# Queries and keys with eight tokens in a row of a partition, transposed head by head

## The chip, the cores and the metric

The kernel runs on one core of a Trainium2 chip. The metric is the device time of one execution in microseconds (us), from the first to the last instruction with what lies around them. Five engines work beside each other: TensorE (PE, matmuls; its weight loads are listed apart as PEld), VectorE (DVE), ScalarE (ACT), GpSimd (POOL) and SyncE (SP, which here only issues transfers). Sixteen DMA engines move the data.

## What is computed

Blockwise causal attention for 8 batches of 8 heads, 576 tokens, 64 values a head, followed by a mixture of experts with one expert a token:

```python
scores = scale * np.matmul(q, k.transpose(0, 1, 3, 2))      # q, k, v: (8, 8, 576, 64) float32
scores = np.where(block_i >= block_j, scores, -1e9)         # blocks of 64 tokens
attn = softmax(scores);  x = attn @ v                       # to (8, 576, 512)
...
e = argmax(x @ w_gate) where the local gate says so, else the expert of the token before
out = p[e] * (relu(x @ w1[e]) @ w2[e])
```

The change touches only the way in which q and k reach TensorE. Scores need both with the 64 values of a head on the partitions and the tokens along the free dimension, so each is loaded with tokens on the partitions and turned by TensorE.

## The kernel before

The attention part works on 32 pairs of heads (`NPR`), four pairs to a batch. It is a software pipeline: the loop `for it in range(-2, NPR)` (L979) handles in one iteration pair `a = it + 2` (turned), `c = it + 1` (maxima and scores), `e = it` (scores, exponentials, products with v) and `x = it - 1` (results stored and turned for the gate). The order of instructions on each engine is the order of the program text; nothing reorders it. After the loop, from about 303 us, come the experts' matmuls, whose weights were loaded during the attention part.

One pair's queries and keys lie in one half of `natb`, a tile [128, 2, 9, 2, 64] in f32 with two buffers: keys on partitions 64 to 127, queries on 0 to 63, then nine blocks of 64 tokens, two heads, 64 values. `load_qk` (L480) fills the first eight blocks. For every pair but the first it issues four transfers on SP, one for queries or keys (`w`) and head (`h`); partition si gets the tokens si, si + 64, si + 128 and so on, 256 B each. The ninth block comes from `load_ends` (L501). `load_qk(a + 2)` is issued when the banks of pair a have been copied out.

In `turns` (L1010) `turn_pair` (L991) transposes the eight blocks for both halves of the partitions: 16 transposes of [64 tokens, 2 x 64 values] into two PSUM banks `pw[0]` (queries) and `pw[1]` (keys), each [128, 512]: 64 partitions for each head, 512 tokens along the row. Pair 0 has its own path on all 128 partitions (L1014 to L1020). ACT copies both banks to `pl` (`turned_in`, L1024 to L1029); copies in bf16 go to `kh` and `qh` (`halves_in`, L1031), from which `top` (L578) computes rough scores, whose maxima DVE takes (L599). `products` (L651, f32), `less` (L659) and `expo` (L668) give the exponentials, `av` (L683) the products with v.

On PE one iteration runs, in order: the middle maxima's scores (L588, L594, L568), two segments of products (L655, L664), the turns (L993), the high maxima's scores (L573), products for the next pair (L655), the tails and the transposes of results (L717, L1050), the low maxima's scores (L573), `less` (L664) and `av` (L689, L697). Once a batch come the gate's sums (L762).

SP issues, each iteration, three transfers for v (L513, L515), the four of `load_qk`, two of `load_ends`, and the rows of x (L533, L538, L540). The experts' weights come through POOL's queue (L63).

Of the kernel before, what the change touches and what calls it, by code (L numbers as in the profile page):

```python
# [16 lines left out]
def kernel(  # L17
# [11 lines left out]
    nc = tc.nc  # L29
# [57 lines left out]
    def rt(shape, dt, name):  # L87
        return rt_p.tile(shape, dt, tag=name, name=name)

    id_f = rt([P, P], F32, "id_f")  # L90
# [352 lines left out]
    with tc.manual_schedule():  # L443
# [33 lines left out]
            "p (m z s d) -> p m z s d", z=2, s=2, d=D)  # L477
        NTWO = NPR - 6

        def load_qk(i, engs=(nc.sync,)):  # L480

            b, hp = divmod(i, HP)
            t = nats[i] = natb[:, i % 2]
            if i:
                for w in (1, 0):
                    for h in range(2):
                        nc.sync.dma_start(out=t[64 * w:64 * w + 64, 0:8, h, :],
                                          in_=(q, k)[w][b, 2 * hp + h, :512].rearrange(
                                              "(so si) d -> si so d", si=64))
                return  # L490
            for z, (w, h) in enumerate(((1, 0), (1, 1), (0, 0), (0, 1), (1, 2), (0, 2))):
                s = (q, k)[w][b, 2 * hp:2 * hp + 2]
                eng = engs[z % len(engs)]
                if h < 2:
                    eng.dma_start(out=t[:, 4 * w:4 * w + 4, h, :],
                                  in_=s[h, :512].rearrange("(so si) d -> si so d", si=128))
                else:
                    eng.dma_start(out=t[64 * w:64 * w + 64, 8],
                                  in_=s[:, 512:S].rearrange("h p d -> p h d"))
# [106 lines left out]
        def rows(h):  # L606
            return slice(64 * h, 64 * h + 64)
# [272 lines left out]


        load_qk(0, (nc.sync, nc.scalar))
        nc.scalar.copy(share[:, 0:1], ones[:, 0:1])
        load_qk(1)
        load_ends(1)
        warm(26)
# [92 lines left out]
        for it in range(-2, NPR):  # L979
# [4 lines left out]
            if it == 0:  # L984
                nc.sync.dma_start(out=wgl[:, :, :E],
                                  in_=moe_w_gate.rearrange("(do di) e -> di do e", di=P))
                for ko in range(KO1):
                    nc.sync.dma_start(out=wgl[:, ko, E:E + 1],
                                      in_=moe_w_local[ko * P:(ko + 1) * P, :])

            def turn_pair(b):  # L991
                for w in range(2):
                    nc.tensor.transpose(pw[w][:, 64 * b:64 * b + 64],  # L993
                                        nat[rows(w), b].rearrange("p h d -> p (h d)"),
                                        id_f[rows(w), rows(w)])

            def weights(n):
                while n:
# [11 lines left out]
            def turns():  # L1010

                pw[:] = g_tile(0), g_tile(1)
                if a == 0:
                    for w in (1, 0):  # L1014
                        for t in range(4):
                            nc.tensor.transpose(pw[w][:, 128 * t:128 * t + 128],
                                                nat[:, 4 * w + t].rearrange("p h d -> p (h d)"),
                                                id_f)
                        turned(0, w, pw[w])
                    return  # L1020
                for b in range(8):
                    turn_pair(b)
# [61 lines left out]
            pw = []  # L1084
            if on_a:
                nat = nats[a]
                pl = pls[a] = plb[:, a % 2]
                mxs[a] = o_p.tile([P, 16], F32, tag="mx", name="mx")
            if it == -2:
                turns()  # L1090
                g1 = tails()
                tails_in()
                load_qk(2)
                load_ends(2)
                top(0, 2, 1)
                low_exchange(0)
                weights(2)
                mid_maxima(0, 2)
                low_shift(0)
                opened = seg_tile(0)  # L1100
                products(0, opened, 0, 0)
                products(0, opened, 0, 1)
                high_maxima(0, 1)
                continue
# [307 lines left out]
```

## Time and profile before

| | |
|---|---|
| median of three runs | 449.35 us (447.96 to 454.55) |
| the profiled execution | 452.64 us, of it 450.9 us from the first to the last instruction |
| granted TensorE clock in it | 0.998 |
| attention part | to about 303 us |
| HBM read and written | 67.18 MB and 14.97 MB |

How to read the rows below: a row of the groups names line, engine, operation, the tile written and the tiles read, the shape (partitions and columns of the array by `64*128`, then partitions x elements), the count, busy us, and the mean ns of one instruction, which on PE includes its way through the array, so that many overlap. A row of the chain of work gives start, duration, engine, tile and line of a piece; the chain is followed back from the last instruction to what released each step. A row of the windows gives for a stretch the busy us of each engine with counts, the granted clock, the share of the DMA engines and GB/s. A row of the timeline gives the start of a merged group and the time to its last end.

### The profile page before, as it was taken

To read this page: it belongs to the slowest core of one execution; us is meant where nothing else is said; L and a number is where in the kernel's file an instruction comes from. 1 tells how busy PE (TensorE), PEld (TensorE's weight loads), DVE (VectorE), ACT (ScalarE), POOL (GpSimd) and SP (SyncE) were. 2 spreads that over 40 slices of the span, in tenths; PEclk is the share of its full clock that TensorE was granted. 3 is DMA by queue.
4 is the path that set the end of the run, shared out by engine and by line. 5 is a ranking of instruction groups with operands and counts; after the bars stand their busy time and mean duration, and the time that the engine had idled before them with its cause. 6 is when DMAs were issued, how large, how long until landed. Compare 5 with 4: busy or idle time off the path is not lost.

```text
span 450.9 us, 19788 instructions
## 1 busy us (share of the span) xinstructions
PE 431.3 (96%) x7802; PEld 338.7 (75%) x7802; DVE 316.2 (70%) x842; ACT 271.0 (60%) x573; POOL 294.2 (65%) x699
## 2 busy tenths in 40 slices
PE   7999999999999999999999999999999999999994
PEld 6687787878787887788778877886776776767772
DVE  5777667768778878897999898857966862433332
ACT  4766665766567757775676666554554553545452
POOL 4656457657556566787766788664777667676752
PEclk9999999999999999999999999999999999999999
DMA  8999689999999997989888898857545746455541
GB/s 154 195 156 188 127 171 183 172 184 165 192 168 172 170 178 152 192 168 186 160 163 172 152 186 159 153 108 165 144 140 154 145 126 156 124 152 145 144 132 63
DMA packets 169887, 71.18 MB, mean 158 GB/s; under 512 B 151424, under 2 KB 158080, under 8 KB 169792
## 3 DMA queue, kind: packets, MB, share of 16 engines
q1 hardware_dynamic: 154640, 38.05, 44.4%
q0 software_dynamic: 13952, 31.52, 34.1%
q8 instruction: 65, 1.06, 1.0%
q10 hardware_dynamic: 1200, 0.30, 0.3%
q14 instruction: 30, 0.25, 0.2%
HBM read 67.18 MB, written 14.97 MB: 182 GB/s over the span
## 4 chain that ended last, share of the span: by engine, by line
PE 61%; DVE 11%; DMA 9%; issue 7%; POOL 6%; ACT 4%; POOLq 1%; ACTq 0%; DVEq 0%
PE g L697 13%; PE ps_s L655 12%; PE ps_h L828 10%; PE ps_o L843 8%; DVE mx L599 5%; PE g L689 4%; DMA out_dram<-o_sb,tok2s 3%; PE ps_s L664 3%; DMA x_rows<-w_bf 2%; PE g L762 2%; PE g L993 2%; POOL out_dram L852 2%; PE ps_m L573 1%; DMA vt<-in_v_dram 1%; PE g L717 1%
## 5 line engine op out<-in xcount | busy, mean ns | idle before, releaser
L671 ACT ACTIVATE prob<-ps_s 128x640 f32<-128x640 f32 (+2 forms) x128 | 103.6, 839 | 45.8 <-PE ps_s L664 42.5
L599 DVE TENSOR_REDUCE mx<-ps_m 128x2 f32<-128x640 f32 (+2 forms) x96 | 100.2, 1044 | 15.2 <-PE ps_m L594 5.6
L655 PE MATMUL ps_s<-plb 64*128 64x320 f32 (+4 forms) x768 | 103.8, 391 | 0.5 <-DVE mx L604 0.2
L655 PEld LDWEIGHTS ps_s<-plb 64*128 64x128 f32 x768 | 68.6, 187 | 21.2 <-issue 11.0
L697 PE MATMUL g<-vt,prob 128*64 128x65 f32 x2560 | 81.5, 222 | 1.1 <-issue 1.1
L697 PEld LDWEIGHTS g<-vt,prob 128*64 128x64 f32 x2560 | 78.1, 138 | 1.8 <-issue 1.7
L843 PE MATMUL ps_o<-w_bf,hT 128*128 x304 | 71.5, 379 | 0.0
L832 ACT ACTIVATE hT<-ps_h 128x512 bf16<-128x512 f32 x76 | 44.0, 597 | 42.1 <-PE ps_h L828 31.1
L809 DVE COPY natb<-w_bf 128x4096 bf16 x20 | 24.7, 1234 | 38.5 <-PE ps_h L828 24.2
L843 PEld LDWEIGHTS <-hT 128*128 128x128 bf16 x304 | 28.0, 98 | 27.8 <-issue 0.3
L846 ACT ACTIVATE o_sb<-ps_o,share 128x512 f32<-128x512 f32 x37 | 25.4, 687 | 28.7 <-PE ps_o L843 14.3
L828 PEld LDWEIGHTS <-plb 128*128 128x128 bf16 x608 | 35.5, 98 | 7.2 <-issue 3.2
L828 PEld LDWEIGHTS <-natb 128*128 128x128 bf16 x608 | 35.4, 98 | 4.6 <-issue 0.7
L664 PE MATMUL ps_s<-diag,ones 64*128 64x448 bf16 (+2 forms) x372 | 37.1, 274 | 1.3 <-DVE diag L618 0.6
L809 DVE COPY plb<-w_bf 128x4096 bf16 x20 | 24.8, 1241 | 15.9 <-PE ps_h L828 13.9
L63 POOL DMA_DIRECT2D w_bf<-in_moe_w_dram x56 | 34.1, 609 | 1.5 <-DMA x_rows<-xb 0.4
L1029 ACT COPY plb<-g 128x512 f32<-128x512 f32 x62 | 33.2, 593 | 0.2
L681 POOL MEMSET prob<- 64x128 f32 x128 | 24.2, 205 | 12.8 <-ACT prob L671 7.4
L612 POOL COPY mx<-mx 64x2 f32<-64x2 f32 x64 | 11.9, 185 | 31.4 <-DVE mx L599 29.8
L852 POOL DMA_INDIRECT out_dram<-o_sb,tok2s x17 | 21.0, 1237 | 16.5 <-ACT o_sb L846 9.1
L689 PEld LDWEIGHTS g<-vt,prob 128*64 128x64 f32 x640 | 21.4, 137 | 10.6 <-ACT xT L725 4.5
L689 PE MATMUL g<-vt,prob 128*64 128x65 f32 x640 | 26.0, 227 | 3.4 <-ACT xT L725 1.2
(290 smaller groups left out, 801.8 us busy)
## 6 DMA issues: line engine op xcount, KB each, us to landing
w_bf<-in_moe_w_dram POOLq DMA_DIRECT2D x48, 256.0 KB
vt<-in_v_dram SPq DMA_DIRECT2D x64, 128.0 KB
natb<-in_k_dram SPq DMA_DIRECT2D x63, 128.0 KB
natb<-in_q_dram SPq DMA_DIRECT2D x63, 128.0 KB
w_bf<-in_moe_w_dram POOLq DMA_DIRECT2D x8, 512.0 KB
x_rows<-w_bf SPq DMA_DIRECT2D x13, 256.0 KB
natb<-in_k_dram SPq DMA_DIRECT2D x32, 32.0 KB
vt<-in_v_dram SPq DMA_DIRECT2D x32, 32.0 KB
```

The source lines that it names most:

```text
L63: nc.gpsimd.dma_start(out=dst[:, e * WE:(e + 1) * WE].rearrange("p (k f) -> p k f", k=n)[:, r:r + m, :], in_=view[e][:, r:r + m, :])
L599: nc.vector.reduce_max(mx[:, 7:12:4] if job == 0 else mx[:, b:b + 2], ps[:, :, 0:w], axis=AX)
L655: nc.tensor.matmul(ps[:, h, c:c + n], lhsT=pls[i][rows(h), S + 128 * j:S + 128 * j + 128], rhs=pls[i][rows(h), a:a + n], start=part == 0, ...
L664: nc.tensor.matmul(ps[:, h, c:c + n], lhsT=ones[rows(h), :], rhs=diag[rows(h), a // 64:(a + n) // 64, :], start=False, stop=part == len(SE ...
L671: nc.scalar.activation(p[:, :, SEG0[s]:SEG0[s] + w], ps[:, :, 0:w], func=AF.Exp, scale=scale_attn)
L689: nc.tensor.matmul(g[rows(h), 130:195], lhsT=p[:, h, c:c + 64], rhs=t[:, j, h, :], start=(j == 0), stop=(j == 4))
L697: nc.tensor.matmul(g[rows(e), o + 65 * h:o + 65 * h + 65], lhsT=p[:, h, c:c + 64], rhs=t[:, j, h, :], start=(j == 0), stop=(j == m))
L809: nc.vector.tensor_copy(w, w1_bf[:, bass.ds(off, WE)])
L828: nc.tensor.matmul(ps_h[:, f, :], lhsT=w[:, f0 + ko * F:f0 + ko * F + 2 * P - 1:2], rhs=xb[:, ko * P:(ko + 1) * P], start=(ko == 0), stop= ...
L832: nc.scalar.activation(hT[:, half * 4:half * 4 + 4, :], ps_h, func=AF.Relu)
L843: nc.tensor.matmul(ps_o, lhsT=hT[:, fo, :], rhs=w2_bf[:, bass.ds(woff + fo * Dm, Dm)], start=(fo == 0), stop=(fo == FO - 1))
L1029: nc.scalar.copy(pl[:, w * S:w * S + 512], pw[w])
```

## The change

The transfers of `load_qk` (for all pairs but the first) and `turn_pair` are rewritten; everything else stays.

```diff
+        def by_head(t):
+            return t[:, 0:8].rearrange("p s h d -> p (s h d)").rearrange("p (h n) -> p h n", h=2)
...
                 for w in (1, 0):
-                    for h in range(2):
-                        nc.sync.dma_start(out=t[64 * w:64 * w + 64, 0:8, h, :],
-                                          in_=(q, k)[w][b, 2 * hp + h, :512].rearrange(
-                                              "(so si) d -> si so d", si=64))
+                    nc.sync.dma_start(out=by_head(t)[64 * w:64 * w + 64],
+                                      in_=(q, k)[w][b, 2 * hp:2 * hp + 2, :512].rearrange(
+                                          "h (si so) d -> si h (so d)", so=8))
...
             def turn_pair(b):
-                for w in range(2):
-                    nc.tensor.transpose(pw[w][:, 64 * b:64 * b + 64],
-                                        nat[rows(w), b].rearrange("p h d -> p (h d)"),
-                                        id_f[rows(w), rows(w)])
+                for h in range(2):
+                    for w in range(2):
+                        nc.tensor.matmul(pw[w][rows(h), b:512:8],
+                                         lhsT=by_head(nat)[rows(w), h, 64 * b:64 * b + 64],
+                                         rhs=id_f[rows(w), rows(w)], start=True, stop=True)
```

The same 4 KB of a partition now hold, for each of the two heads, eight consecutive tokens (8 si to 8 si + 7) as one run of 2 KB, read from one run of 2 KB in memory. One transfer brings both heads, 256 KB. A turn b takes the b-th token of each of the 64 partitions, of one head, and puts them in every eighth column of the bank, so that the banks hold the tokens in the same order as before. Input and output of such a turn are 64 partitions each, a quarter of the array; it is an f32 matmul with the identity in place of a transpose. There are 32 of them for a pair in place of 16 transposes.

## The prediction

> **What bounds the kernel now.** I read the page first (span, slices, the shares of the chain of work that ended last), then the windows by stage, then the chain over one iteration, and last the groups by shape.
>
> ```profile
> span 450.9 us, 19788 instructions
> ...
> PE 431.3 (96%) x7802; PEld 338.7 (75%) x7802; DVE 316.2 (70%) x842; ACT 271.0 (60%) x573; POOL 294.2 (65%) x699
> ...
> PE 61%; DVE 11%; DMA 9%; issue 7%; POOL 6%; ACT 4%; POOLq 1%; ACTq 0%; DVEq 0%
> PE g L697 13%; PE ps_s L655 12%; PE ps_h L828 10%; PE ps_o L843 8%; DVE mx L599 5%; PE g L689 4%; DMA out_dram<-o_sb,tok2s 3%; PE ps_s L664 3%; DMA x_rows<-w_bf 2%; PE g L762 2%; PE g L993 2%; POOL out_dram L852 2%; PE ps_m L573 1%; DMA vt<-in_v_dram 1%; PE g L717 1%
> ```
>
> PE is busy for 96% and makes up 61% of the chain, transfers 9%. The lines of the change are L993 (2% of the chain) and the loads, which stand on the chain nowhere.
>
> ```profile
> 20.00:56.00 36.00, 34.71 (x740) 28.28 (x737) 25.35 (x65) 23.30 (x53) 20.28 (x68) 1.00 0.94 163
> 56.00:92.00 36.00, 35.59 (x792) 29.41 (x790) 25.76 (x67) 24.59 (x56) 23.16 (x75) 1.00 1.00 176
> 92.00:128.00 36.00, 34.58 (x750) 28.14 (x744) 27.49 (x75) 23.76 (x54) 22.71 (x74) 1.00 1.02 177
> ...
> 237.00:274.00 37.00, 35.83 (x776) 29.34 (x776) 33.85 (x99) 25.10 (x59) 27.61 (x86) 1.00 0.91 171
> ```
>
> The columns are PE, PEld, DVE, ACT, POOL busy, granted clock, DMA share, GB/s. In the attention stage PE works up to 35.6 of 36 us with the DMA engines at 1.00 beside it; late in the stage DVE (33.9 of 37) comes close. One iteration of the chain (start, duration) shows what PE does:
>
> ```profile
> 82.53 0.80 PE g L689 x20
> 83.33 2.33 PE g L697 x80
> ...
> 87.39 0.49 PE g L993 x16
> 87.89 0.22 PE ps_m L573 x2
> 88.11 1.68 PE ps_s L655 x16
> 89.78 0.31 PE g L717 x10
> ...
> 90.79 0.21 ACT scr L725
> ...
> 91.04 0.80 PE g L689 x20
> ```
>
> An iteration takes 91.04 - 82.53 = 8.51 us and is a row of PE pieces without a hole, closed by ACT's copies after the tails. The sixteen transposes of turn_pair (L993) hold 0.49 of it. Whatever they cost more is added to the iteration, unless another engine is later anyway.
>
> **The change part by part.** First, what the new turn is made of.
>
> ```profile
> L697 PE MATMUL g<-vt,prob 128*64 128x65 f32 x2560 | 81.5, 222 | 1.1 <-issue 1.1
> ...
> L655 PE MATMUL ps_s<-plb 64*128 64x320 f32 x256 | 44.2, 430 | 0.0
> ...
> L993 PE MATMUL g<-id_f,natb 64*128 64x64 f32 x496 | 20.9, 222 | 0.1
> ...
> L664 PE MATMUL ps_s<-diag,ones 64*128 64x320 bf16 x124 | 18.6, 296 | 0.0
> ...
> L573 PE MATMUL ps_m<-kh,qh 64*128 64x512 bf16 x64 | 12.2, 376 | 0.2
> ...
> L762 PE MATMUL g<-xT,wgl 128*32 128x160 f32 x64 | 5.9, 305 | 0.0
> ...
> L709 PE MATMUL g<-id_f,x 128*64 128x64 f32 x4 | 0.3, 246 | 0.0
> ```
>
> A transpose is one instruction: 31 turned pairs (the first pair has its own path) x 16 = 496. An f32 matmul, an identity one too, is two: L709 is called twice in the whole kernel and shows x4, and L697 is 32 pairs x 40 calls x 2 = 2560. So 16 transposes become 32 matmuls of a quarter of the array, 64 instructions with 64 weight loads, 16 for each quarter.
>
> What one costs, and how many run at once, is read in the timeline (start, span of the merged group):
>
> ```profile
> 85.32 0.34 PE L697 MATMUL g<-vt,prob 128*64 128x65 f32 x6
> 85.59 0.20 PE L588 MATMUL ps_m<-kh,qh 64*128 64x64 bf16 x2
> ```
> ```profile
> 58.59 0.47 PE L762 MATMUL g<-xT,wgl 128*32 128x160 f32 x8
> ```
>
> Eighty L697 in 2.33 us are 29 ns each; as its two column halves work side by side, one half takes 58 ns for 65 columns. The L762 row has eight matmuls of about 0.3 us inside 0.47 us: two rounds of four, on four column strips at once. Quarters (two row halves by two column halves) appear nowhere. The bounds: all four at once, 16 rounds x 58 = 0.93 us; two at once, 32 x 58 = 1.86 us. I take 0.93, since both kinds of halves and even four strips overlap here, and each half of the rows then streams what L697 streams. Removed: 0.49.
>
> Next, the shape of the array changes before and after the turn (now 64*128 like its neighbours L664 and L573). The six L697 above are three pairs (0.34 - 0.222 = two steps of 58 ns), the last from 85.44; the next would have been due at 85.50, but L588, of another shape, begins at 85.59: 0.09 to 0.10 us lost. Two such changes are new: +0.19 (bounds 0, if a quarter counts as the same shape, and 0.2). [...]
>
> So a turn goes from 0.49 to 1.12: +0.63 us on PE. What is queued behind it on PE is the top job (L573) and the products (L655); ACT waits with its copies out of the turned banks (L1026 to L1029), and POOL and DVE behind those; all move by the same amount.
>
> How many of the 31 pay? The chain holds 2.0% of 450.9 = 9.0 us of L993, 18 turns of 0.49. In the other 13 another engine is later, for example:
>
> ```profile
> 243.24 0.38 PE L573 MATMUL ps_m<-kh,qh 64*128 64x512 bf16 x2
> ```
> ```profile
> 244.44 1.14 DVE mx L599
> ```
>
> PE has the scores that this maximum reads at 243.62, DVE takes them up at 244.44: 0.82 us of room, as DVE is busy with other work. Room in the 13 lies between 0 and 0.82; I take 0.5, nearer to this row. Sum: 18 x 0.63 + 13 x 0.13 = 11.3 + 1.7 = 13.0 us (bounds for the room: 11.3 and 19.5).
>
> Then the loads. Four transfers a pair become two, 512 runs of 256 B each become 128 of 2 KB.
>
> ```profile
> q1 hardware_dynamic: 154640, 38.05, 44.4%
> q0 software_dynamic: 13952, 31.52, 34.1%
> ...
> natb<-in_k_dram SPq DMA_DIRECT2D x63, 128.0 KB
> ```
> ```profile
> L487 SPq DMA_DIRECT2D natb<-in_k_dram x62: 595/626/1218, 2.7 to 264.3; - x62
> ```
>
> 31 x 4 x 512 = 63488 of the queue's 154640 packets become 31 x 2 x 128 = 7936. A packet of q1 costs 0.444 x 16 x 450.9 / 154640 = 20.7 ns for 246 B; q0's, 2.26 KB on average, 176 ns. Per byte these are alike, so a 2 KB run may save nothing, or up to most of 63488 x 20.7 / 16 = 82 us of each engine; SP saves two issues of 0.63 us a pair. Either way the loads stand off the chain. What a lighter queue can reach are three pieces in which something else waited for a transfer:
>
> ```profile
> 31.63 6.04 DMA vt<-in_v_dram
> ...
> 43.84 5.16 DMA x_rows<-w_bf
> ...
> 115.27 5.88 DMA x_rows<-w_bf
> ```
>
> Here PE mostly went on with other work: in the windows 20 to 56 and 92 to 128, which hold the three pieces, it was idle 1.3 and 1.4 of 36 us, against 0.4 in 56 to 92. So at most 0.9 + 1.0 = 1.9 us can come back; I take 0.8 of 0 to 1.9, since the turns that grow fill part of the same holes. Nothing changes after 303 us, where the loads are over. Sum: +13.0 - 0.8 = +12.2. The profiled execution took 452.64 us, span 450.9, so it would take 464.8; the median of the three runs is 3.3 us below that execution, so I forecast 449.35 + 12.2 = 461.5 us.
>
> **The rivals.**
> Issue. The new turn wants 128 PE instructions in 0.93 us, 7 ns each. The narrowest stream of the trace is slower:
>
> ```profile
> 330.29 0.67 PE g L391 x27
> ```
>
> That is 25 ns for a matmul with its load, so 64 need 1.6 us. A turn then costs 1.6 + 0.19 - 0.49 = +1.30: 18 x 1.30 + 13 x 0.80 - 0.8 = +33, 482 us. Against it: L391 uses the whole array, and where two row halves take turns, six short matmuls start between 85.59 and 85.69, 17 ns each:
>
> ```profile
> 85.59 0.23 PE L588 MATMUL ps_m<-kh,qh 64*128 64x64 bf16 x4
> 85.66 0.19 PE L594 MATMUL ps_m<-kh,qh 64*128 64x64 bf16 x2
> 85.69 0.19 PE L568 MATMUL ps_m<-ones,unseen 64*128 64x64 bf16 x2
> ```
>  [...]
>
> Slow columns. The outputs are strided, every eighth f32 of a bank; every PE output of the trace lies in runs. If a strided column costs twice, 16 rounds cost 16 x 116 = 1.86 us, which is also the case of two quarters at once: +1.56 a turn, 18 x 1.56 + 13 x 1.06 - 0.8 = +41, 490 us. [...] For the other side: f32 columns come slowly already, (430 - 222) / 255 = 0.8 ns each by the rows of L655 and L697, against (376 - 296) / 192 = 0.4 for the bf16 ones of L573 and L664, so there may be time for one write each.
>
> No change. The shape change costs nothing and the queue's relief is whole: 18 x 0.44 - 1.9 = +6.0, 455 us (+1.3%), the 13 others absorbing 0.44 within 0.5.
>
> Faster. The full DMA engines set the pace after all, and the three pieces above, 17.1 us of the chain, vanish: 449.35 - 17.1 + 7.9 = 440 us. It decides only if all of the 17.1 goes; PE busy for 34.7 and 34.6 of 36 us in the windows that hold them speaks against.
>
> **How the numbers follow.** Quarters concurrent with two shape changes: 43 in 100, 461.5 us, own range 458 to 469. Issue 15 (482), slow columns or two at once 20 (490), no change 18 (455), faster 4 (440). The range 453 to 490 leaves out faster, the lowest part of no change and what would lie above both upper bounds. A measurement here tells about 2% (9 us) from no change. Faster by over 2%: 0.04; within 2%: 0.20 (no change, and the low edge of the first); slower by over 2%: 0.76.
>
> **What would show it.** The turn's line with 31 x 64 = 1984 matmuls, PE with 7802 + 1488 = 9290; the turn's piece of the chain about 1.1 us from the last L664 to the top job: 1.0 would take the shape changes away, 1.8 or more speaks for issue (if even starts 25 ns apart) or for slow columns (if each quarter's own step is above 58 ns). An undisturbed iteration goes from 8.51 to 9.1 us. q1 falls to 99088 packets; if the three transfer pieces stay, the lighter queue was worth nothing. Wrong it would be above all if the quarters do not overlap, or if iterations get shorter although PE does more.

## The result, and the profile after

The changed kernel takes 470.03 us against 448.26 us for the kernel before, medians of seven runs each; the ratio is 1.0446 (95% interval 1.0401 to 1.0492). Run again it came to 1.0501 (1.0472 to 1.0530), 477.82 against 455.24 us. It is slower by 20 to 23 us. The ratios take only the runs at the usual clock, and as the first profile of the changed kernel was taken at a granted clock of 0.655, the rows below are those of the second run, e0_after, at 0.996 (span 473.5 us). Its lines are numbered two to three higher than before. Beside it stands a second profile of the kernel before (b0_before, span 452.2 us). It comes from another chip than e0_after, but the kernel before takes 455.24 us in the median on the one and 455.29 on the other.

The page of the changed kernel:

```profile
span 473.5 us, 22616 instructions
...
PE 448.7 (95%) x9268; PEld 351.1 (74%) x9290; DVE 319.4 (67%) x842; ACT 273.7 (58%) x573; POOL 296.3 (63%) x699
...
q1 hardware_dynamic: 98096, 38.05, 36.9%
q0 software_dynamic: 13952, 31.52, 33.7%
q8 instruction: 76, 1.25, 1.1%
...
PE 68%; issue 12%; POOL 7%; ACT 5%; DMA 3%; DVE 3%; POOLq 1%; another core or an unknown queue 1%; DVEq 0%; ACTq 0%
PE ps_s L657 18%; PE g L699 15%; PE g L996 7%; PE g L691 5%; PE ps_h L830 4%; POOL out_dram L854 3%; PE ps_o L845 3%; DMA out_dram<-o_sb,tok2s 3%; PE ps_m L575 2%; PE ps_s L666 2%; POOL scr L795 2%; PE g L764 2%; PE g L719 2%; POOL xg L795 2%; ACT plb L1062 2%
```

The same of b0_before:

```profile
q8 instruction: 65, 1.06, 1.0%
...
PE 62%; issue 10%; DVE 8%; POOL 8%; DMA 6%; ACT 5%; POOLq 1%; ACTq 0%; DVEq 0%
```

PE issues 9290 weight loads in place of 7802, the 1488 more that were worked out, and the turn's line is 7% of the chain in place of 2% (3% in b0_before). DVE has gone from 11% of the chain (8% in b0_before) to 3%, and transfers from 9% (6%) to 3%. "Issue", time in which the engine waits for nothing that the profile shows, is 12% where the two profiles of before have 7% and 10%; between 20 and 300 us it is 2.4% of the chain, against 2.3% in b0_before, so most of it lies behind the part that was changed. The queue q1 has 56,544 packets fewer.

One plain iteration of the chain, to be held against the one of before:

```profile
63.64 1.09 PE g L996 x64
64.73 0.32 PE ps_m L575 x2
65.06 1.68 PE ps_s L657 x16
66.73 0.31 PE g L719 x10
...
67.18 0.27 ACT plb L1062
...
67.99 0.80 PE g L691 x20
68.80 2.33 PE g L699 x80
...
72.86 1.09 PE g L996 x64
```

It takes 72.86 - 63.64 = 9.22 us; it was 8.51. All other pieces are as long as before. The turn went from 0.49 to 1.09, and the piece of the top job behind it from 0.22 to 0.32. That is +0.70 us in every plain iteration, one in which no other engine is late.

The windows (PE, PEld, DVE, ACT, POOL busy, clock, DMA share, GB/s), first of the kernel before (b0_before), then of the changed one:

```profile
56.00:92.00 36.00, 35.61 (x784) 29.38 (x780) 26.29 (x68) 24.81 (x57) 23.12 (x73) 1.00 1.02 177
92.00:128.00 36.00, 35.42 (x775) 29.11 (x774) 29.57 (x77) 24.94 (x58) 23.71 (x76) 1.00 0.99 184
```
```profile
56.00:92.00 36.00, 34.75 (x884) 28.26 (x880) 23.41 (x62) 21.97 (x50) 21.05 (x68) 1.00 0.82 159
92.00:128.00 36.00, 35.12 (x890) 28.53 (x888) 26.68 (x70) 23.89 (x55) 21.46 (x69) 1.00 0.83 167
```

The DMA engines, which looked full at 1.02 and 0.99, are at 0.82 and 0.83, and nothing became faster by it. PE is idle for 1.25 us in the first of these windows, against 0.4 before: part of the loss is holes in PE's work, which e4_twice and e6_shift are about.

### The profile page after: what moved, and what is told of

Same layout as the page of the kernel before. It is cut to its first block, busy times and chain, and to the rows that moved or that the text cites. A ratio compares the mean times of both kernels' runs of the same rounds, so it can differ in the third digit from the quotient of the medians.

```text
span 632.4 us, 22638 instructions
## 1 busy us (share of the span) xinstructions
PE 624.3 (99%) x9290; PEld 449.9 (71%) x9290; DVE 324.6 (51%) x842; ACT 276.7 (44%) x573; POOL 290.0 (46%) x699
## 3 DMA queue, kind: packets, MB, share of 16 engines
q8 instruction: 76, 1.25, 0.8%
## 4 chain that ended last, share of the span: by engine, by line
PE 86%; issue 6%; DMA 4%; POOL 3%; POOLq 0%; DVE 0%; ACTq 0%; DVEq 0%
PE ps_s L657 21%; PE g L699 17%; PE ps_h L830 10%; PE ps_o L845 10%; PE g L996 7%; PE ps_s L666 5%; PE g L691 5%; PE ps_m L575 3%; DMA out_dram<-o_sb,tok2s 3%; PE g L764 2%; PE g L719 2%; PE ps_m L596 1%; POOL out_dram L854 1%; POOL xg L795 1%; PE ps_m L590 1%
## 5 line engine op out<-in xcount | busy, mean ns | idle before, releaser
L657 PE MATMUL ps_s<-plb 64*128 64x320 f32 (+4 forms) x768 | 148.8, 520 | 0.0
L657 PEld LDWEIGHTS ps_s<-plb 64*128 64x128 f32 x768 | 77.9, 200 | 45.4 <-issue 19.8
L699 PEld LDWEIGHTS g<-vt,prob 128*64 128x64 f32 x2560 | 109.2, 176 | 0.3 <-issue 0.3
L845 PE MATMUL ps_o<-w_bf,hT 128*128 x304 | 105.4, 512 | 0.0
L830 PEld LDWEIGHTS <-natb 128*128 128x128 bf16 x608 | 49.8, 119 | 8.0 <-issue 5.9
L830 PEld LDWEIGHTS <-plb 128*128 128x128 bf16 x608 | 50.0, 119 | 7.5 <-issue 6.1
L996 PEld LDWEIGHTS g<-id_f,natb 64*64 64x64 f32 x1984 | 41.5, 170 | 18.4 <-issue 18.1
L666 PE MATMUL ps_s<-diag,ones 64*128 64x448 bf16 (+1 forms) x372 | 47.6, 356 | 0.0
L996 PE MATMUL g<-id_f,natb 64*64 64x64 f32 x1984 | 47.4, 257 | 0.0
L614 POOL COPY mx<-mx 64x2 f32<-64x2 f32 x64 | 11.6, 181 | 70.9 <-DVE mx L601 69.4
L1037 POOL CAST qh<-plb 128x512 bf16<-128x512 f32 x30 | 18.3, 609 | 48.8 <-ACT plb L1032 48.8
L830 PE MATMUL ps_h<-scr,natb 128*128 128x128 bf16 x416 | 36.3, 265 | 0.0
```

What stands on the lines that cost most here:

```text
L657: nc.tensor.matmul(ps[:, h, c:c + n], lhsT=pls[i][rows(h), S + 128 * j:S + 128 * j + 128], rhs=pls[i][rows(h), a:a + n], start=part == 0, ...
L666: nc.tensor.matmul(ps[:, h, c:c + n], lhsT=ones[rows(h), :], rhs=diag[rows(h), a // 64:(a + n) // 64, :], start=False, stop=part == len(SE ...
L699: nc.tensor.matmul(g[rows(e), o + 65 * h:o + 65 * h + 65], lhsT=p[:, h, c:c + 64], rhs=t[:, j, h, :], start=(j == 0), stop=(j == m))
L830: nc.tensor.matmul(ps_h[:, f, :], lhsT=w[:, f0 + ko * F:f0 + ko * F + 2 * P - 1:2], rhs=xb[:, ko * P:(ko + 1) * P], start=(ko == 0), stop= ...
L845: nc.tensor.matmul(ps_o, lhsT=hT[:, fo, :], rhs=w2_bf[:, bass.ds(woff + fo * Dm, Dm)], start=(fo == 0), stop=(fo == FO - 1))
L996: nc.tensor.matmul(pw[w][rows(h), b:512:8], lhsT=by_head(nat)[rows(w), h, 64 * b:64 * b + 64], rhs=id_f[rows(w), rows(w)], start=True, sto ...
```

## The experiments

**e0_after.** The changed kernel, no edit.

> The changed kernel as it is, for a profile at a full granted clock. Turn theory (PE's longer turn makes all of the loss): ratio to before 1.045 as measured; the piece from the last L666 to the top job's first L575 is 1.1 us against 0.49, and a plain iteration goes from 8.51 to 9.1 us. Rival, the loads (2 KB runs cost time somewhere, or relieve it): the turn's piece is 1.1 us but the iterations or the waits for vt and x_rows change by more than that. Rival, the clock: the granted clock stays under 0.99 and the experts' part, which the change does not touch, is longer too.

Ratio 1.0501. A group row and a row of the timeline show how the quarters run:

```profile
L996 PE MATMUL g<-id_f,natb 64*64 64x64 f32 x1984 | 37.0, 221 | 2.8 <-issue 2.8
```
```profile
24.66 0.34 PE L996 MATMUL g<-id_f,natb 64*64 64x64 f32 x8
```

Eight matmuls of about 0.22 us within 0.34 are two rounds of four. In the trace four start 7 ns apart, and the next four follow after a step that is 58 ns in the median; only the first step of a turn is longer, 107 ns: there the weight loads start 2 ns ahead of their matmuls, in later rounds 56 ns. So 107 + 15 x 58 = 0.98 us. Where the shape of the array changes, 0.09 us are lost ahead of the turn (226 ns from the start of the last L666 to the first L996, 132 from L664 to L993 before) and 0.11 us behind it (the top job starts 171 ns after the last round, 58 would be a step). Together this is 1.18 us; the 1.09 of the piece and the 0.10 more of the top job are 1.19. This is the turn theory's piece.

The rest is in three turns out of 31, of which this is the first (timeline, with PE's idle time and its cause in brackets):

```profile
82.01 0.92 PE L996 MATMUL g<-id_f,natb 64*64 64x64 f32 x46
83.52 0.56 PE L996 MATMUL g<-id_f,natb 64*64 64x64 f32 x18 [0.59 <-issue]
84.02 0.39 PE L575 MATMUL ps_m<-kh,qh 64*128 64x512 bf16 x2
```

After 46 of its 64 matmuls the turn stops for some 0.8 us and goes on. Nothing that it computes with is late. It happens again after 61 and after 29 matmuls, for 1.3 and 1.2 us.

**e1_loads.** The new loads with the old transposes (of blocks that now mix tokens, so that it computes the attention of other queries and keys).

```diff
+                    nc.sync.dma_start(out=by_head(t)[64 * w:64 * w + 64],
+                                      in_=(q, k)[w][b, 2 * hp:2 * hp + 2, :512].rearrange(
+                                          "h (si so) d -> si h (so d)", so=8))
```

> The loads of the change alone, with the sixteen transposes of before; the blocks then mix tokens of one head, so the result is that of other queries and keys. Turn theory: same time as before within 0.5%, at most 2 us faster (ratio 0.996 to 1.000), as the transfers stand off the chain. Rival, the loads matter: outside of 0.99 to 1.01.

Ratio 1.0035 (1.0009 to 1.0061), just above what I expected. The loads alone bring nothing; if anything they cost 0.35%. Its two windows:

```profile
56.00:92.00 36.00, 35.04 (x776) 28.99 (x771) 25.70 (x67) 24.14 (x55) 22.89 (x73) 1.00 0.92 183
92.00:128.00 36.00, 35.36 (x779) 29.09 (x774) 29.55 (x77) 24.92 (x58) 23.62 (x76) 1.00 0.85 169
```

The DMA share falls from 1.02 and 0.99 to 0.92 and 0.85, and PE is not busier by it. The 0.35% need not be the loads' doing: this trace has four of the holes that are explained at e4_twice, 3.9 us against 1.1 in b0_before, and without them both take 252 us from the third turn to the last. So the relief that I had put at 0.8 us is not there, and the rival that the full DMA engines set the pace falls.

**e2_turns.** The quarter turns on the old loads, so that each output is a run of 64 columns.

```diff
-                for w in range(2):
-                    nc.tensor.transpose(pw[w][:, 64 * b:64 * b + 64],
-                                        nat[rows(w), b].rearrange("p h d -> p (h d)"),
-                                        id_f[rows(w), rows(w)])
+                for h in range(2):
+                    for w in range(2):
+                        nc.tensor.matmul(pw[w][rows(h), 64 * b:64 * b + 64],
+                                         lhsT=nat[rows(w), b, h, :],
+                                         rhs=id_f[rows(w), rows(w)], start=True, stop=True)
```

> The 32 quarter turns alone, on the loads of before; their outputs are runs of 64 columns and not every eighth column. Turn theory: ratio 1.04 to 1.05 as with the whole change, turn piece 1.1 us. Rival, strided outputs cost: the turn piece is shorter here than in the whole change by 0.1 us or more. Rival, the loads relieve: ratio higher than with the whole change by 0.5% or more.

Ratio 1.0527 (1.0487 to 1.0567), the interval overlaps that of the whole change. The chain has the same piece:

```profile
63.55 1.09 PE g L994 x64
64.64 0.32 PE ps_m L573 x2
```

1.09 us with outputs in runs, 1.09 with every eighth column: the strided outputs cost nothing here, and the turns alone make the whole loss.

**e3_halves.** The transposes of before as plain f32 matmuls with the identity, both heads at once, no change of shape.

```diff
-                    nc.tensor.transpose(pw[w][:, 64 * b:64 * b + 64],
-                                        nat[rows(w), b].rearrange("p h d -> p (h d)"),
-                                        id_f[rows(w), rows(w)])
+                    nc.tensor.matmul(pw[w][:, 64 * b:64 * b + 64],
+                                     lhsT=nat[rows(w), b].rearrange("p h d -> p (h d)"),
+                                     rhs=id_f[rows(w), rows(w)], start=True, stop=True)
```

> The loads of before, and sixteen f32 identity matmuls of both heads in place of the sixteen transposes: 32 instructions in 16 rounds of two, and the shape of the array does not change around them. If the two shape changes cost 0.19 us a turn: turn piece 0.93 to 1.0 us and 18 to 31 times 0.19, that is 3.4 to 5.9 us, less than with quarter turns (ratio 1.03 to 1.037). If they cost nothing: the same time as with quarter turns.

Ratio 1.0717 (1.0687 to 1.0747), far over what I expected, and slower than the quarters.

```profile
65.79 1.73 PE g L993 x32
67.52 0.22 PE ps_m L573 x2
```

Sixteen rounds of two take 1.73 us, 108 ns a round, although each moves the same 64 columns as a quarter does in 58. What differs is the weights: 128 columns of f32 a matmul here, 64 in a quarter. The weight loads take 188 ns here and 135 in the quarters, and start 56 ns after the matmuls ahead of them, where the quarters' loads start 3 ns after theirs. As a transpose the same 128 columns went in 62 ns (0.49 us for eight rounds of two), with loads of 139 ns; why they are quicker there stays open. So this kernel doesn't isolate the price of the shape change, and shows another one. That it is the width of the f32 weight load is the likely reading, and was not tried by itself.

**b0_before.** The kernel before, no edit, for a profile on the chip of the next three.

> The kernel before, unchanged, for a profile on the same chip as the next three. If the longer part behind the last turn (about 174 us in the four kernels run so far, 171 us in the first profile of before) belongs to the chip, it is 173 to 175 us here too; if it belongs to the changes, 171.

From the last turn to the end it needs 172.6 us; the first profile of before has 171.0, e0_after 173.8. That is between the two answers, and the same code takes from 173.1 (e2_turns) to 176.9 us (e6_shift) in the other runs, so what makes it longer stays open. Of the 21.3 us between the spans of b0_before and e0_after 1.2 lie there; the rest belongs to the attention part.

**e5_shape.** The kernel before with one tiny quarter matmul ahead of each pair's transposes.

```diff
+                nc.tensor.matmul(pw[0][0:64, 0:1], lhsT=id_b[0:64, 0:64], rhs=id_b[0:64, 0:1],
+                                 start=True, stop=True)
                 for b in range(8):
                     turn_pair(b)
```

> The kernel before with one tiny quarter-array matmul (64 by 64 weights, one column, bf16) ahead of each pair's sixteen transposes; its value is overwritten by them. It adds two shape changes and next to no work. Shape changes cost 0.1 us each: plain iteration 8.51 to 8.7 to 8.8 us, ratio 1.008 to 1.015. They cost nothing: ratio 1.000 to 1.003.

Ratio 1.0155 (1.0119 to 1.0191).

```profile
70.85 0.12 PE g L1021
70.96 0.64 PE g L993 x16
71.61 0.22 PE ps_m L573 x2
```

A single one-column matmul lengthens the turn from 0.49 to 0.76 us and the plain iteration to 8.78: +0.27 for two changes of shape. Ahead of the tiny matmul 0.09 us are lost; the transposes start 0.12 us after it, and their first step takes 0.11 in place of 0.06. The price that the prediction took from L588's late start is shown, and is a little more than was taken.

**e4_twice.** The changed kernel with every quarter matmul issued twice.

```diff
-                for b in range(8):
-                    turn_pair(b)
+                for b in range(16):
+                    turn_pair(b % 8)
```

> The changed kernel with each turn's 32 quarter matmuls issued twice over (the second pass writes the same values again), no further change of the array's shape. If PE's time passes on whole: 16 more rounds of 58 ns are +0.93 us a turn, plain iteration 9.22 to 10.15 us, 31 x 0.93 = +29 us, ratio 1.11 to 1.12. If other engines' lateness still absorbs part: under +20 us. If 256 instructions in a row outrun PE's issue: rounds longer than 58 ns and more than +35 us.

Ratio 1.1619 (1.1552 to 1.1686): 528.0 us, 50 us more than the changed kernel, where 29 were expected of PE's time and more than 35 only if the rounds became longer. They don't: the step is 58 ns in the median again, and an undisturbed iteration takes 10.15 us as worked out. Of the other 21 us some 18 are holes (chain of work; the row with q8 is from the page):

```profile
52.00 1.04 PE g L996 x70
53.03 2.61 issue
55.65 0.34 PE g L996 x7
```
```profile
q8 instruction: 92, 1.51, 1.2%
```

q8, which the page calls instruction, has 65 packets in the kernel before (each of 16,384 B in its trace), 76 in the changed one, 92 here. PE has 2976 and 6944 more loads and matmuls than in the kernel before, and q8 gained 11 and 27 packets: 271 and 257 instructions a packet. At 256 each, the number that the counting at e6_shift gives too, they would be 11.6 and 27.1 packets. Listed from the traces, eight of the holes of the attention part, with the time since the last q8 packet had landed when PE went on:

```
kernel      PE goes on at   hole, us   packet landed before that, us
b0_before   157.53          0.40       1.34
e0_after     83.52          0.76       1.39
e0_after    201.78          1.33       1.49
e0_after    279.78          1.20       1.52
e2_turns    203.30          1.40       1.35
e4_twice     55.65          2.78       1.35
e4_twice    201.39          2.72       1.26
e4_twice    303.10          1.81       1.46
```

Every time PE goes on 1.3 to 1.5 us after a packet of instructions has come. Gaps between two matmuls that are at least 0.15 us longer than the usual one there are five in e0_after from 20 us on (4.5 us over the usual in all), ten in e2_turns and 20 in e4_twice. But for one each in the last two, all end 1.2 to 1.7 us after a packet; these are 5.5 us in e2_turns and 22.7 us in e4_twice. In b0_before only two of ten do (1.1 us). Of the others, most show a wait for another engine; one of 0.6 us at 293.87, behind the last turn, comes 3.5 us after a packet and stays unexplained. A turn of e4_twice has 256 instructions by itself: 128 loads and 128 matmuls in 2.0 us.

**e6_shift.** The changed kernel with 64 more PE instructions ahead of everything.

```diff
         warm(26)
+        for _ in range(32):
+            nc.tensor.matmul(warm_ps[:, 0:1], lhsT=ones, rhs=ones[:, 0:1], start=True, stop=True)
```

> The changed kernel with 32 one-column matmuls (64 PE instructions) more in the warm-up ahead of the first loads' landing. Theory that PE's holes in the middle of a turn (up to 1.3 us, after 46, 61 and 29 of its 64 matmuls) come from a late block of instructions: they move by 32 matmuls to earlier places, inside the turn after 14 and 29 or out of it, and again end 1.3 to 1.5 us after an instruction packet has landed. Theory that something the turn itself waits for (a load, a bank) causes them: they stay in the same turns and places. Total within 0.5% of the changed kernel, ratio 1.045 to 1.055.

Ratio 1.0473 (1.0430 to 1.0516). No turn is interrupted any more. Four holes are left, 1.7 us in all, one right behind a turn and three in other lines, such as this one, again 1.7 us after a packet:

```profile
80.05 0.51 PE g L691 x9
80.56 0.28 issue
80.83 0.51 PE g L691 x10
```

So the holes moved with the stream of instructions, and are not set by what the turn waits for. The traces show it by counting, too. Number PE's loads, matmuls and semaphore instructions in the order of their starts: after each of the 43 holes that so follow a packet in b0_before, e0_after, e1_loads, e2_turns, e4_twice and e6_shift, PE goes on at a number that leaves 193 when it is divided by 256. I had expected the first two holes a little earlier in the same turns, after 14 and 29 matmuls. By the count such places lie there now, but PE passes them 2.7 and 2.3 us after the packet, and goes on. At no such place of these traces does it pass less than 1.2 us after it.

From the third turn to the last the kernel takes 271.8 us against 275.0, 3.2 less, where its holes are 2.9 us less. Its third turn comes 2.7 us later and its part behind the last turn takes 3.2 us more, so the total is about the same. b0_before, without the added matmuls, has its third turn at 26.3 us, e6_shift at 27.3 and e0_after at 24.7, so the later start need not be theirs.

## Why the prediction was right, and where its sizes were off

I forecast 461.5 us, +12.2; measured are 470.03 and +21.8 by the medians (+20 by the ratio). The range of 453 to 490 holds it; the main case's own, 458 to 469, just misses it. The direction, the mechanism and its place held; the sum was short by 8 to 10 us, and its terms can be held against the trace.

*What bounds it.* PE did: the turn's added time went into nearly every iteration, and a DMA share that fell from 1.02 and 0.99 to 0.92 and 0.85 by the loads alone was worth nothing (e1_loads, ratio 1.0035).

*Two instructions for each f32 matmul, 16 rounds of 58 ns.* Right: 1984 matmuls, step 58 ns, four quarters at once. Of the bounds 0.93 and 1.86 us the lower one was the case.

*Two changes of shape, 0.19 us.* The holes are 0.09 and 0.11 us. Missed was the first round behind a change, 107 ns in place of 58. The turn with what follows costs +0.70, not +0.63: over 31 turns 2 us more. By itself e5_shape shows 0.27 us for the pair of changes with the tiny matmul between them and the longer first step behind them.

*Thirteen turns with 0.5 us of room.* This step failed by its size. The count of 18 turns on the chain came from a rounded 2%, which is 3% in b0_before. The room I read where DVE takes up a maximum (0.82 us), but what an iteration can swallow is at most how much longer it already is than a plain one. Take the 28 iterations from the third turn to the last, b0_before against e0_after: 253.3 and 275.0 us. The plain lengthening is 28 x 0.71 = 19.8 us of the 21.7. In seven iterations the time over plain shrinks, by 3.1 us in all, of which 1.1 are holes for instructions that b0_before has at other places. So 2 us were swallowed, where I had counted 13 x 0.5 = 6.5. In others, PE now meets ACT before `av`, which the late DVE had hidden: the gaps from the last L664 to the first L689 add up to 11.5 us in place of 9.0.

*The lighter loads, 0.8 us.* Nothing. The count of packets was right but for 992, 16 of 4 B for each of the 62 transfers that are gone.

*Not in the sum: holes for instructions.* They grew by 3.4 us in that stretch, from 1.1 to 4.5. This term belongs to the one stream of instructions as much as to the change: with the same turns e6_shift has 1.7 us of them. The rival "Issue" took the 25 ns of L391 for a floor between starts, and e0_after goes below it: the quarters of a round start 7 ns apart, 14.5 ns in the mean with the step between rounds, well under 25. What came with more instructions are these holes instead; in e4_twice they are 20 us in that stretch.

Together: 2 + 4.5 + 0.8 + 3.4 = 10.7 us, somewhat more than what was missing. The rival "Slow columns", whose doubled step of 116 ns was an assumption, is wrong for this kernel: e2_turns (outputs in runs) and e0_after (every eighth column) show the same 1.09 us in f32; a bf16 matmul wasn't tried. No kernel here beats the one before: in the changed layout a token's values for the two heads lie 2 KB apart, its turn goes head by head, and the loads that this pays for were not worth anything.

## What to carry to other kernels

A resource that shows a share of 1.0 bounds a kernel only if the chain of waits goes through it; emptying the DMA engines from 1.02 and 0.99 to 0.92 and 0.85 bought nothing here (e1_loads, ratio 1.0035), while PE, on the chain in nearly every iteration, passed on the 0.27 us of e5_shape and the 0.70 us of e0_after whole to a plain iteration. Splitting a TensorE step into smaller tiles cost more here than its columns: two instructions for each f32 matmul (64 for the 32 of a turn, 1984 in all), 0.09 and 0.11 us at the two changes of the array's shape, a first round of 107 ns in place of 58, whose weight loads start only 2 ns ahead of their matmuls (e0_after), and holes of 4.5 us in place of 1.1 from the third turn to the last. The room of an iteration is not the wait of one engine in it; it is at most how much longer the iteration is than the shortest one, and less where PE itself does more in it or another wait was hidden.

## What the runs showed of the hardware

Holes of 0.3 to 2.8 us in the middle of PE's work end 1.2 to 1.7 us after a 16 KB packet of q8 has landed. All 43 of six traces lie where the count of PE's instructions leaves 193 when it is divided by 256, and in e6_shift, with 64 instructions more ahead, they lie elsewhere in the program. Call 256 counted instructions a block. In b0_before, where a block lasts 6.1 us in the median, the holes are 1.1 us; in e0_after a block lasts 5.1 us and the holes are 4.5 us, in e4_twice 4.8 and 22.7. The length of a block is not all of it: e1_loads has 6.3 us a block and 3.9 us of holes. In e0_after a packet starts 1.6 us (median) after PE has passed the end of the block before, but 2.5 to 3.8 us ahead of the five holes. What makes it start late wasn't tried.

A round of two f32 matmuls with 128 weight columns each takes 108 ns (e3_halves), one of two transposes with as many 62 ns (0.49 us for eight rounds, the kernel before), one of four f32 matmuls with 64 weight columns each 58 ns (e0_after).
